# Linear attention and a rational FFN on one core: a new order table for the same instructions

## The chip, the cores and the metric

The kernel runs on one core of a Trainium2 chip. Its engines are TensorE (PE in the profile, PEld for its weight loads), VectorE (DVE), ScalarE (ACT), GpSimd (POOL) and SyncE (SP, which issues the DMAs). Each works through a queue of its own in order, and they meet at semaphores. The metric is device time in microseconds: the median of 3 runs, 544.45 us before (541.43, 544.45 and 544.65).

## The reference

```python
# attention: r, k, v (4, 8, 768, 48); w, u (8, 48)
for t in range(S):
    cur = np.einsum('bhd,bhe->bhde', u[None] * kt, vt)
    y[:, :, t] = np.einsum('bhd,bhde->bhe', rt, state + cur)
    state = w[None, :, :, None] * state + np.einsum('bhd,bhe->bhde', kt, vt)
# FFN over x = y as 3072 tokens x 384
h = x @ w_in                                   # 384 -> 2048
P = a[0] + a[1] * h + a[2] * h**2 + a[3] * h**3
Q = 1.0 + np.abs(b[0]) * np.abs(h) + np.abs(b[1]) * h**2
return (P / (Q + 1e-06)) @ w_out               # 2048 -> 384
```

The weights w_in and w_out arrive as 64-bit floats, so they are converted on the chip.

## The kernel before

**Attention.** The 3072 tokens are 24 blocks of 128; two blocks make a pair (m = 0 to 11). For a block n the kernel loads r, k and v (`rh`, `kh`, `vn`), forms the bonus term (`m`: r*k, times u, summed to `dt`, times v), scales k and r by powers of w (`wkn`, `wrn`), transposes them on PE (L513) and copies them out (`kt`, `rt`). For a pair PE forms `kv` (L562), the masked products `a` (L541, `av` after the mask of L549) and `y` in two parts (L591: with the state, then with `av` and v). DVE adds y to `m` (L607, two halves for each block); PE transposes the sum (`x`, L619), and it is kept as a high and a low half (`xth`, `xtl`).

**Weights.** They come in 28 pieces, loaded to `sti` and `sto`: in each of four groups three of w_in (512 wide, "i", 512 KB) and four of w_out (384 wide, "o", 384 KB). ACT splits a piece (L392, L380, L383), DVE joins it to a single-precision `wfi` or `wfo` (L397), ACT or DVE casts the high half (L420, `whii`, `whio`), and POOL or DVE subtracts for the low half (L417, `wloi`, `wloo`).

**FFN.** A token tile is a pair's 256 tokens. Its 2048 hidden columns are eight slices of two times 128; the first two tiles share each quarter of the weights (slices 0 and 1 of tile 0, 2 and 3 of tile 1, 4 and 5 of tile 0 again, and so on), later tiles go through in one run. Slice s: PE's product `h` (L644 in three products of halves, or L650 in full precision for tile 0), then ACT (|h| L692, `w` L698, `t` L703, ln L708, exp L712), then DVE (L716, `g` high half L722, `q` L726, the remainder d L732), then the low half of g on POOL or DVE (L736), then PE's second product into `o` (L654 to L656), which takes the low half as the third of its operands. `o` is evicted at the end of a quarter or a tile (L778, L783, L785) and stored.

**What sets the order.** The kernel is cut into 2205 tasks, each a few instructions. `ORDER` is a table of their numbers: it is the program order of all engines together, and a letter behind a number picks the engine where a task may run on two (D is DVE, A ACT, G POOL, S a DMA from SP). A token such as `w1` puts a product of ones on PE, whose result is not used. `placed` reads the table and refuses an order in which a task stands ahead of what it depends on, or a buffer runs out:

```python
for tok in ORDER.split():
    if tok[0] == "w":
        order += [("warm", "P")] * int(tok[1:])
        continue
    n = names[int(tok.rstrip(ENGINES))]
    t = tasks[n]
    e = tok[-1] if tok[-1] in ENGINES else t["eng"]
```

**The scale constants.** `pro_beta` takes the absolute values of a and b on ACT (L260, L261), clamps two of them on DVE (L264, `ctmp`), takes a root through ln and exp on ACT (L265, L266) and sets four constants on DVE (L267 to L270); `pro_squares` follows with 14 tiny DVE instructions. ACT's `t` and `w` of every slice need them.

Of the kernel before, what the change touches and what calls it, by code (L numbers as in the profile page):

```python
# [48 lines left out]
69 286D 70D 71G 789 790 791 288D 283 77D 793 93 94 792 803 804 293G 294G 291 278 304 43G 284G 95 794 796 296 96 795 97 797 798
799 800G 309D 805 128 129 130 807 131 132 806 w1 324 100 101 808 102 103 298 300 301D 310 299D 810 104 801 802 78G 323 326G 329G  # L50
297G 327G 114 107 809 115 116 117 303A 811 812 813 814G 305 307 306 308 328D 108 302A 109 110 133A 118 119A 111 312 313 319 314
815 334 318 315 332 336 325 337 339G 342G 343 121 122 123 124 335A 333A 226 227 338 316D 320 321A 317 125 126A 228 340G 345 346D
341G 347 348D 149 150 322 330 351 356 352 229 230 151 816A 152 135 136 137 57G 50G 819 820 821 112D 357 354 98D 153 91D 105D 353
355 138 139 822 154D 823 826 817 818D 824 825 827 828 829 170 350S 171 349S 833 834 837 127G 113G 331G 359 360 361 172 835 173
174 344G 849 850 836 838 365 840 140D 366 212 213 863 864 384 466 142 830G 831 839 841 842 843 99D 832 844D 845 847 851 214 852
215 216 854 865 853 856 855 857 858 848D 143 866 144 868 106G 92G 120G 162G 859 860G 145 146 846D 867 870 147D 869 871 872 385
219 220 417 177 383 879 880 881 893 861 372 371 134G 883 886 873 874G 882 221 884 222 223 885 887 888 175D 889 231D 890G 894 909
895 178 897 896 179 900 910 911 180 898 912 862 875 877 876 181 217D 182D 183G 878 923 924 141G 899 901 902 913 916 914 903 904D
163 164 191 925 165 915 166 917 192 926 193 928 194 167 168A 927 891 892 905 918 906 919 195 907 908 929 930 931 932 933 184 185
155G 148G 939 940 941 953 954 186 943 946 920G 169G 921 218G 176G 934D 922 935 187 198 199 942 200 201 188 196D 202 937 938 944  # L60
945 947 948 949 950G 957 955 956 936 958 959 960 961 962 969 970 983 971 984 197G 203A 189A 985 986 988 987 989 951 963 964D 972
974 362 363D 364 990 991 952 965 967 992 993 367 368A 369 190G 204G 1001 1002 1015 1016 1033 973 976 975 977 978 968 979 966 205
206 224A 207 208 1003 1005 386G 232G 388G 994G 387G 980G 1004 1006 1007 209 1008 210D 211D 1009 1010 1019 1034 1047 370 373G
225D 1017 1022 1018 1020 1021 394 395D 1011 1023 1048 981 1024 982 995 998 999 996 1025 397S 419 1061 1012G 389G 374D 1026G 1051
1037 1049 1035 1050 1052 1054 1053 1055 1056 1057 1058G 1062 1065 1036 1063 1038 1039 1064 392 393A 1040 1041 1042 1043 1044G
1013 1014 1027 1066 1067 1068 1069 1030 1075 1076 1079 1089 1090 1103 513 1000 1070 1031 1032 1028 1071 1072G 1077 1078 1082 379
1080 1081 1083 1084 376G 375G 358G 1104 1117 1045 1118 1046 1059 1060 1073 1093 377 1091 1092 390 1096 1085 1086D 1105 1094 1095
1097 1098 380A 391D 311G 1099 1100 1107 1119 1106 1120 1110 1108 1109 1111 1112 1121 1122 1123 1074 1087 1131 1132 1133 381 418
382A 1088 1101 1102 1113 1114 1115 1134 1136 1124 1125 1126 1127 1128 1135 1137 1138 1139 1140 398 399 403 400 1116 401 396S 431
402 406 1141 378G 407 408 1129 420G 421G 409 410A 1130 1142 412 404 413 411 414 415A 430 433G 435G 441 432 442A 426 427A 422G  # L70
428 465 464 429A 416 1149 1150 1163 1164 434G 423G 424 445 450 477 1151 1152 1153 1156 451 1167 1165 1166 1168 1170 1169 1171
1172 1173 1174 436G 1143 1144A 1154 1155 1157 1158 1159 437 439 511 560 1146 1147A 1177 1178 1179 478 1148 1181 1191 1192 1205
# [1016 lines left out]
```

## Time and profile before

| | |
|---|---|
| median of 3 runs | 544.45 us (541.43 to 544.65) |
| the profiled execution | 542.21 us, of which the span is 540.4 |
| PE, PEld busy | 510.0, 490.7 us |
| DVE, ACT, POOL busy | 427.9, 404.5, 250.0 us |
| HBM read, written | 27.73, 4.72 MB |

The span goes from the first to the last instruction of the program; the profiled execution's time is 1.8 us longer. Busy time is the union of an engine's instructions. PE's products overlap in the records, so two products that follow each other closely each show a duration longer than their distance.

### The profile page before, as it was taken

How to read it: one execution, taken by the hardware profiler on the slowest of the kernel's cores; microseconds unless marked ns; L12 is line 12 of the kernel's file. 1: busy time of each engine (PE TensorE's matmuls, PEld its weight loads, DVE VectorE, ACT ScalarE, POOL GpSimd, SP SyncE). 2: the span in 40 equal slices, each digit the busy share in tenths (PEclk: the TensorE clock that was granted, in tenths of full speed). 3: DMA queues.
4: the chain of work that ended last, by engine and by line, in shares of the span. 5: the costliest groups of instructions: out<-in, count | busy, mean ns of one | idle time of the engine just before them, and what ended most of it. 6: DMA issues, size and time to landing. Idle time of an engine off the chain costs nothing.

```text
span 540.4 us, 14734 instructions
## 1 busy us (share of the span) xinstructions
PE 510.0 (94%) x6055; PEld 490.7 (91%) x6055; DVE 427.9 (79%) x708; ACT 404.5 (75%) x666; POOL 250.0 (46%) x241
## 2 busy tenths in 40 slices
PE   4758999899999999999999999999999999999995
PEld 2647988899999999999999999999999899999995
DVE  5889999899974887887796868789867785776872
ACT  5789999998864857948963857876785785788782
POOL 3669545384444662551563654235523432222331
PEclk9899999999999999999999999999999999999999
DMA  8967642240022311104304232040031000000001
GB/s 205 267 172 202 183 112 76 79 80 16 16 52 50 79 32 45 31 4 89 81 2 91 52 76 52 2 81 2 2 82 32 1 30 2 2 30 1 29 2 35
DMA packets 88492, 33.46 MB, mean 62 GB/s; under 512 B 81761, under 2 KB 84834, under 8 KB 88418
## 3 DMA queue, kind: packets, MB, share of 16 engines
q1 hardware_dynamic: 88418, 32.46, 25.4%
q8 instruction: 49, 0.80, 0.6%
q14 instruction: 25, 0.20, 0.1%
HBM read 27.73 MB, written 4.72 MB: 60 GB/s over the span
## 4 chain that ended last, share of the span: by engine, by line
PE 76%; DVE 5%; ACT 4%; DMA 1%; issue 1%; POOL 0%; DVEq 0%; POOLq 0%; ACTq 0%; SPq 0%
PE h L644 30%; PE o L654 11%; PE o L656 11%; PE o L655 11%; PE y L591 3%; PE h L650 2%; PE kv L562 2%; PE a L541 2%; PE tr L513 2%; PE tk L513 2%; PE x L619 1%; DVE q L726 1%; DVE g L722 1%; ACT w L698 1%; DVE h L716 1%
## 5 line engine op out<-in xcount | busy, mean ns | idle before, releaser
L736 POOL TENSOR_TENSOR g<-q,z 128x512 fp32r<-128x512 f32 (+1 forms) x92 | 118.5, 1289 | 234.4 <-DVE q L732 142.9
L644 PE MATMUL h<-xth,whii 128*128 128x256 f32 x528 | 151.2, 286 | 0.1
L644 PE MATMUL h<-xtl,whii 128*128 128x256 f32 x528 | 148.0, 280 | 0.0
L644 PE MATMUL h<-xth,wloi 128*128 128x256 f32 x528 | 148.0, 280 | 0.0
L654 PE MATMUL o<-whio,g 128*128 128x384 f32 x384 | 134.5, 350 | 0.0
L656 PE MATMUL o<-whio,g 128*128 128x384 f32 x384 | 130.3, 339 | 1.9 <-DVE g L736 1.9
L655 PE MATMUL o<-wloo,g 128*128 128x384 f32 x384 | 129.9, 338 | 0.0
L698 ACT ACTIVATE w<-q,off,root 128x512 f32<-128x512 f32 (+1 forms) x97 | 75.4, 779 | 48.5 <-DVE q L726 22.5
L644 PEld LDWEIGHTS h<-xth,whii 128*128 128x128 f32 x528 | 99.4, 188 | 1.7 <-DVE q L726 0.9
L644 PEld LDWEIGHTS h<-xtl,whii 128*128 128x128 f32 x528 | 99.5, 188 | 0.0
L644 PEld LDWEIGHTS h<-xth,wloi 128*128 128x128 f32 x528 | 99.4, 188 | 0.0
L722 DVE SCALAR_TENSOR_TENSOR g<-h,sig,z 128x512 fp32r<-128x512 f32 (+1 forms) x97 | 72.1, 743 | 33.7 <-ACT z L712 29.2
L716 DVE SCALAR_TENSOR_TENSOR h<-t,sig,h 128x512 f32<-128x512 f32 (+1 forms) x97 | 71.9, 743 | 15.6 <-ACT t L703 9.7
L703 ACT ACTIVATE t<-h,off,root 128x512 f32<-128x512 f32 (+1 forms) x97 | 74.3, 767 | 6.8 <-PE h L644 6.6
L726 DVE SCALAR_TENSOR_TENSOR q<-w,sig,g 128x512 f32<-128x512 f32 (+1 forms) x97 | 72.2, 744 | 6.3
L656 PEld LDWEIGHTS o<-whio,g 128*128 128x128 f32 x384 | 72.1, 188 | 3.2 <-DVE g L736 2.9
L732 DVE SCALAR_TENSOR_TENSOR q<-h,sig,q 128x512 f32<-128x512 f32 (+1 forms) x97 | 72.0, 744 | 2.7
L654 PEld LDWEIGHTS o<-whio,g 128*128 128x128 f32 x384 | 72.1, 188 | 1.0
L655 PEld LDWEIGHTS o<-wloo,g 128*128 128x128 f32 x384 | 72.3, 188 | 0.1
L692 ACT ACTIVATE q<-h 128x512 f32<-128x512 f32 (+1 forms) x97 | 56.2, 584 | 20.7 <-PE h L644 19.7
L712 ACT ACTIVATE z<-z,lnb 128x512 f32<-128x512 f32 (+1 forms) x97 | 69.7, 719 | 2.2
L708 ACT ACTIVATE z<-w,lnb 128x512 f32<-128x512 f32 (+1 forms) x97 | 66.0, 680 | 6.9 <-POOL g L736 2.6
(141 smaller groups left out, 664.9 us busy)
## 6 DMA issues: line engine op xcount, KB each, us to landing
sti<-in_moe_w_in_dram SPq DMA_DIRECT2D x12, 512.0 KB, 5.1
sto<-in_moe_w_out_dram SPq DMA_DIRECT2D x16, 384.0 KB, 3.8
rh<-in_r_dram SPq DMA_DIRECT2D x24, 192.0 KB, 3.5
kh<-in_k_dram SPq DMA_DIRECT2D x24, 192.0 KB, 4.0
vn<-in_v_dram SPq DMA_DIRECT2D x24, 192.0 KB, 4.4
out_dram<-os SPq DMA_DIRECT2D x24, 192.0 KB, 2.1
vo<-in_v_dram SPq DMA_DIRECT2D x10, 96.0 KB, 3.9
wraw<-in_w_dram SPq DMA_DIRECT2D x1, 1.0 KB, 2.5
```

The lines of the kernel that those rows point to most:

```text
L644: nc.tensor.matmul(o, w_[nm][:, c], x_[:, cc], start=(n == 0), stop=(n == 3 * NCC - 1))
L654: nc.tensor.matmul(o, hi, w_["hi"], start=first, stop=False)
L655: nc.tensor.matmul(o, hi, w_["lo"], start=False, stop=False)
L656: nc.tensor.matmul(o, lo, w_["hi"], start=False, stop=last)
L698: nc.scalar.activation(g["w"], w_, AF.Square, scale=RB, bias=KB)
L703: nc.scalar.activation(g["t"], g["h"], AF.Square, scale=RA, bias=KA)
L712: nc.scalar.activation(g["z"], g["z"], AF.Exp, scale=-1.0, bias=lnb[:, 1:2])
L716: nc.vector.scalar_tensor_tensor(g["h"], g["t"], KAP, g["h"], op0=ALU.add, op1=ALU.mult)
L722: nc.vector.scalar_tensor_tensor(g["hi"], g["h"], c0, g["z"], op0=ALU.add, op1=ALU.mult)
L726: nc.vector.scalar_tensor_tensor(g["q"], g.get("w", g["q"]), qe, g["hi"].bitcast(F32), op0=ALU.add, op1=ALU.mult)
L732: nc.vector.scalar_tensor_tensor(g["d"], g["h"], c0, g["q"], op0=ALU.add, op1=ALU.subtract)
L736: e.tensor_mul(g["lo"], g["d"], g["z"])
```

## The change

Only the table `ORDER` is replaced. All tasks and their instructions stay, with two kinds of exception that the table itself sets: where a task may run on two engines, its letter may differ, and there are 12 tokens for a product of ones instead of 4. Of the whole program's choices, v's half copies go from 11 on ACT, 3 on DVE and 10 as a DMA to 9, 3 and 12; the casts of the high halves of weights from 10 on ACT and 18 on DVE to 6 and 22; the low halves of weights from 25 on POOL and 3 on DVE to 27 and 1; the low halves of g from 92 and 5 to 91 and 6; the scaling of k from 21 and 3 to 18 and 6. Nearly every task's place in the order is another one. The list of loads, which was r of block 0, w, two weight pieces, k of block 0, u, a weight piece, r and k of block 1, a weight piece, is now a weight piece, w, two weight pieces, k of both blocks, r of block 1, a weight piece, r of block 0, u. The new table was searched under a planner's model in which DVE and POOL are served in order of arrival at a port that they share.

```diff
 ORDER = """
-234 0 35 12 13 14 16 18 15 17 20 19 21 5 4 7 22 23 27 44 45 46 47 58 233 59 60 61 1 10 24 25 3 243 30 28 48 236G 11 238G 239 6
...
+58 59 0 35 60 7 w1 12 13 14 16 61 44 45 15 27 4 18 17 20 19 37 233 3 6 241 28 62 21 46 47 48 22 25 23 242 245 246 248G 63A 38 39
...
```

**At the scale constants, DVE.** y0 is the first pair's y, m1 the second block's sum, x0 and x1 the two transposes, wfi1_0 and wfo1 joins of weight pieces. Before:

```order
L607 TENSOR_TENSOR m1_205<-y0_1_325,m1_205 128x4x48
L607 TENSOR_TENSOR m1_205<-y0_0_324,m1_205 128x4x48
L420 COPY xth0_425<-x0_398 128x3x128
L420 COPY xth0_425<-x1_427 128x3x128
L397 SCALAR_TENSOR_TENSOR wfi1_0_439<-cp7_433,upi1_0_436 128x512
L264 TENSOR_SCALAR ctmp_96<-cabs_95 128x2
```

In the change:

```order
L607 TENSOR_TENSOR m1_185<-y0_1_325,m1_185 128x4x48
L397 SCALAR_TENSOR_TENSOR wfo1_414<-cp4_408,upo1_410 128x384
L264 TENSOR_SCALAR ctmp_96<-cabs_95 128x2
L267 MEMSET sqs_429 128x1
L268 MEMSET sqs_429 128x1
L269 MEMSET lnb_87 128x1
L270 MEMSET lnb_87 128x1
L607 TENSOR_TENSOR m1_185<-y0_0_324,m1_185 128x4x48
L420 COPY xth0_440<-x0_402 128x3x128
L420 CAST whio1_446<-wfo1_414 128x384
L420 COPY xth0_440<-x1_442 128x3x128
```

The clamp (ctmp) and the four constants now stand ahead of the last sum of m1 and of both copies of x; the 14 instructions of `pro_squares` follow the join of wfi1_0 in both.

**From d of slice 0 (q0, L732) on, DVE.** st1 is the second pair's state, vo1 its copy of v, wfo7 and wfo5 joins, kt and rt the copies of transposed k and r. Before, up to d of slice 1:

```order
L732 SCALAR_TENSOR_TENSOR q0_516<-h0_509,sig_97,q0_516 128x512
L420 COPY st1_109<-kv1_0_544 112x384
L397 SCALAR_TENSOR_TENSOR wfo7_609<-cp13_602,upo7_604 128x384
L420 COPY rt_106<-tr3_629 112x512
L573 TENSOR_TENSOR st1_109<-kv1_1_545,st1_109 112x384
L420 COPY kt_105<-tk3_624 112x512
L716 SCALAR_TENSOR_TENSOR h1_531<-t1_606,sig_97,h1_531 128x512
L397 SCALAR_TENSOR_TENSOR wfi1_2_638<-cp9_617,upi1_2_621 128x512
L722 SCALAR_TENSOR_TENSOR g1_674<-h1_531,sig_97,z1_619 128x512
L726 SCALAR_TENSOR_TENSOR q1_598<-w1_611,sig_97,g1_674 128x512
L732 SCALAR_TENSOR_TENSOR q1_598<-h1_531,sig_97,q1_598 128x512
```

In the change the first 12 rows of that stretch; eight more follow (the second half copies of vo1, a cast, r*k of block 5, and g, q and d of slice 1 among them) before d of slice 1 is done:

```order
L732 SCALAR_TENSOR_TENSOR q0_518<-h0_451,sig_97,q0_518 128x512
L736 TENSOR_TENSOR g0_563<-q0_518,z0_526 128x512
L397 SCALAR_TENSOR_TENSOR wfi1_1_587<-cp8_554,upi1_1_577 128x512
L420 COPY vo1_111<-vn2_569 64x192
L420 COPY vo1_111<-vn3_547 64x192
L716 SCALAR_TENSOR_TENSOR h1_499<-t1_633,sig_97,h1_499 128x512
L420 COPY st1_109<-kv1_0_591 112x384
L420 CAST whio8_637<-wfo8_531 128x384
L573 TENSOR_TENSOR st1_109<-kv1_1_592,st1_109 112x384
L397 SCALAR_TENSOR_TENSOR wfo5_686<-cp11_642,upo5_645 128x384
L549 TENSOR_TENSOR av_107<-a1_0_651,mask_81 128x512
L397 SCALAR_TENSOR_TENSOR wfo7_722<-cp13_649,upo7_689 128x384
```

The low half of g0, two half copies of v and a cast of a weight's high half have come in, the copies of kt and rt have gone to ACT, and the masks (L549) of the second pair now stand ahead of d of slice 1.

**Ahead of the transpose of x20, DVE.** m20 and m21 are the sums of the eleventh pair, y10 its y. Before, from the d of slice 70 on:

```order
L716 SCALAR_TENSOR_TENSOR h71_5858<-t71_6075,sig_97,h71_5858 128x512
L607 TENSOR_TENSOR m21_5325<-y10_0_5910,m21_5325 128x4x48
L490 TENSOR_TENSOR rh0_100<-rh0_100,wrn_90 128x8x48
L494 TENSOR_TENSOR m23_6117<-rh1_102,kh2_104 128x384
L607 TENSOR_TENSOR m20_5376<-y10_1_5911,m20_5376 128x4x48
L722 SCALAR_TENSOR_TENSOR g71_6125<-h71_5858,sig_97,z71_6121 128x512
L716 SCALAR_TENSOR_TENSOR h72_6002<-t72_6127,sig_97,h72_6002 128x512
L726 SCALAR_TENSOR_TENSOR q71_5886<-w71_6078,sig_97,g71_6125 128x512
L732 SCALAR_TENSOR_TENSOR q71_5886<-h71_5858,sig_97,q71_5886 128x512
L607 TENSOR_TENSOR m21_5325<-y10_1_5911,m21_5325 128x4x48
L607 TENSOR_TENSOR m20_5376<-y10_0_5910,m20_5376 128x4x48
```

In the change:

```order
L716 SCALAR_TENSOR_TENSOR h70_5855<-t70_6014,sig_97,h70_5855 128x512
L607 TENSOR_TENSOR m20_4994<-y10_1_5918,m20_4994 128x4x48
L607 TENSOR_TENSOR m21_5587<-y10_1_5918,m21_5587 128x4x48
L607 TENSOR_TENSOR m21_5587<-y10_0_5917,m21_5587 128x4x48
L607 TENSOR_TENSOR m20_4994<-y10_0_5917,m20_4994 128x4x48
L722 SCALAR_TENSOR_TENSOR g70_6102<-h70_5855,sig_97,z70_6016 128x512
```

The four sums now stand together behind one L716; before, a scaling, a product r*k and four slice steps lay between them.

## Rows read from the trace of the kernel before

**Rows 1.** The first part of the page: busy time of each engine, its share of the span and its instructions.

```profile
PE 510.0 (94%) x6055; PEld 490.7 (91%) x6055; DVE 427.9 (79%) x708; ACT 404.5 (75%) x666; POOL 250.0 (46%) x241
```

**Rows 2.** Busy time by stretch: the stretch in us, its length, then busy us (and instructions) of PE, PEld, DVE, ACT and POOL, the mean granted clock of PE, the DMA share and GB/s.

```profile
0.00:22.00 22.00, 12.00 (x220) 9.36 (x220) 14.85 (x30) 15.26 (x30) 11.49 (x27) 1.00 0.96 234
22.00:30.00 8.00, 7.05 (x55) 5.89 (x56) 5.55 (x10) 3.02 (x10) 5.77 (x7) 0.57 0.99 230
30.00:48.00 18.00, 10.78 (x198) 8.81 (x196) 16.62 (x43) 17.55 (x34) 12.57 (x13) 1.00 0.64 160
48.00:80.00 32.00, 30.77 (x480) 28.19 (x480) 31.48 (x57) 31.05 (x56) 19.31 (x18) 1.00 0.62 167
80.00:105.00 25.00, 22.36 (x128) 20.69 (x129) 22.47 (x37) 23.06 (x41) 11.53 (x10) 1.00 0.32 91
105.00:534.00 429.00, 426.40 (x4975) 417.43 (x4974) 336.89 (x533) 313.45 (x499) 189.37 (x169) 1.00 0.17 36
```

**Rows 3.** Who waited for whom, PE's own waits: the engine and line that waited, what it waited for, us in total, times, the longest.

```profile
PE h L650 <- DVE wfo L397: 3.0, 1, 3.0
PE tk L513 <- DVE q L732: 2.6, 1, 2.6
PE y L591 <- issue: 2.2, 3, 1.1
...
PE o L656 <- DVE g L736: 1.9, 2, 1.0
PE x L619 <- DVE m L607: 1.8, 2, 1.0
```

**Rows 4.** The timeline from 24 to 31 us, of DVE, of ACT and of POOL: start, duration, engine, line, operation, out<-in, shape, and in brackets the idle time before it with what ended it.

```profile
27.64 1.94 DVE L264 TENSOR_SCALAR ctmp<-cabs 128x2 f32<-128x2 f32 x1
...
30.28 0.17 DVE L277 RECIPROCAL sqs<-root 128x2 f32<-128x2 f32 x1
...
24.30 0.51 ACT L420 CAST whio<-wfo 128x384 fp32r<-128x384 f32 x1 [2.17 <-DVE wfo L397]
...
29.61 0.17 ACT L265 ACTIVATE sqs<-ctmp 128x2 f32<-128x2 f32 x1 [2.78 <-DVE ctmp L264]
...
27.60 0.99 POOL L499 TENSOR_TENSOR m<-m,ub 128x384 f32<-128x384 f32 x1
28.55 0.99 POOL L494 TENSOR_TENSOR m<-rh,kh 128x384 f32<-128x384 f32 x1
```

**Rows 5.** The timeline from 60 to 69 us: two casts of the same form on DVE, and what POOL ran beside the second.

```profile
60.98 0.41 DVE L420 CAST whii<-wfi 128x512 fp32r<-128x512 f32 x1
...
66.64 1.10 DVE L420 CAST whii<-wfi 128x512 fp32r<-128x512 f32 x1
...
66.17 2.70 POOL L417 TENSOR_TENSOR wloi<-wfi,whii 128x512 fp32r<-128x512 f32 x2
```

**Rows 6.** DVE's instructions of the first 105 us, grouped by line and form: line, operation, names, form and count, then busy us, mean ns of one, and idle time before them.

```profile
L716 DVE SCALAR_TENSOR_TENSOR h<-t,sig,h 128x512 f32<-128x512 f32 x11 | 8.2, 746 | 1.0 <-ACT t L703 1.0
...
L420 DVE CAST whii<-wfi 128x512 fp32r<-128x512 f32 x9 | 5.8, 651 | 0.0
...
L736 DVE TENSOR_TENSOR g<-q,z 128x512 fp32r<-128x512 f32 x3 | 3.1, 1032 | 0.0
...
L420 DVE CAST whio<-wfo 128x384 fp32r<-128x384 f32 x8 | 2.9, 373 | 0.0
...
L420 DVE COPY rt<-tr 112x512 f32<-112x512 f32 x3 | 2.1, 684 | 0.3 <-PE tr L513 0.3
L420 DVE COPY kt<-tk 112x512 f32<-112x512 f32 x3 | 2.0, 680 | 0.0
...
L785 DVE TENSOR_SCALAR os<-o,sig 128x384 f32<-128x384 f32 x3 | 1.8, 606 | 0.0
...
L417 DVE TENSOR_TENSOR wloi<-wfi,whii 128x512 fp32r<-128x512 f32 x1 | 1.2, 1223 | 0.0
...
L490 DVE TENSOR_TENSOR rh<-rh,wrn 128x384 f32<-128x384 f32 x1 | 0.7, 704 | 0.0
```

**Rows 7.** The same grouping over the whole run, three forms on DVE and one on ACT.

```profile
L508 DVE TENSOR_TENSOR m<-vn,dt 128x384 f32<-128x384 f32 x5 | 4.1, 817 | 0.0
...
L420 DVE COPY vo<-vn 64x192 f32<-64x192 f32 x6 | 2.8, 497 | 0.1
L494 DVE TENSOR_TENSOR m<-rh,kh 128x384 f32<-128x384 f32 x5 | 2.8, 550 | 0.0
...
L420 ACT CAST whio<-wfo 128x384 fp32r<-128x384 f32 x7 | 3.4, 506 | 2.2 <-DVE wfo L397 2.2
```

**Rows 8.** The timeline around the transpose of x20, of DVE and of PE.

```profile
423.01 0.75 DVE L732 SCALAR_TENSOR_TENSOR q<-h,sig,q 128x512 f32<-128x512 f32 x1
423.68 0.61 DVE L607 TENSOR_TENSOR m<-y,m 128x192 f32<-128x192 f32 x2
...
423.02 0.28 PE L644 MATMUL h<-xtl,whii 128*128 128x256 f32 x1
423.14 0.28 PE L644 MATMUL h<-xth,wloi 128*128 128x256 f32 x1
424.44 0.52 PE L619 MATMUL x<-ident,m 128*128 128x128 f32 x3 [1.01 <-DVE m L607]
```

**Rows 9.** The timeline of DVE at the d of slices 0 and 1.

```profile
39.79 0.75 DVE L732 SCALAR_TENSOR_TENSOR q<-h,sig,q 128x512 f32<-128x512 f32 x1
...
46.30 0.75 DVE L732 SCALAR_TENSOR_TENSOR q<-h,sig,q 128x512 f32<-128x512 f32 x1
```

More of the change, by code (lines that the diff above doesn't have):

```diff
@@ L49 @@
[L49 to L72, printed above, removed]
@@ new lines @@
+811 812 813 312 313 318 347 334 319 314 348A 340G 345 346A 315 316A 111 104 119D 814G 815 320 335D 321D 317 121 325 122 123 124
+338 351 226 227 322 134G 266G 356 357 125 105D 228 229 230 112D 149 150 151 152 817 50G 819 820 823 821 822 824 352 329G 126D
+330 331G 153 354 818D 353 355 98D 342G 343 344G 833 479 120G 113G 127G 231D 350S 135 136 137 825 826 349S 359 366 360 361 365
+138 139 827 828 829 830G 834 835 849 850 837 840 385 170 171 212 836 172 838 863 864 99G 92G 106G 173 851 839 816D 853 852 174
@@ new lines @@
+1436 1449 575G 499G 1467 1469 1472 1468 1470 1471 1473 1474 1475 585A 584S 586 591 565 576G 538S 620 547 549 554 548 592 582
+583D 563G 569 1377 606 608G 580 581A 1450 567 618 714 619 607 631S 632S 550 570A 588 568A 587 553 577D 578 551D 552 555 556A
+579D 1479 1480 1483 1481 557 589 1497 590 594 609D 614 1462 1463 566D 611D 612 596 600 595 615A 1486 601 1482 1484 1485 1487
+1488 597 598A 613G 1498 1511 1512 1464 621G 1476 1477 599 1489 622D 610G 616 617D 1499 1500 1502 1501 1504 1525 1503 1515 1505
@@ new lines @@
+1538 676 713 677D 1551 1596 1552 593G 1564 1565 657G 669G 663 1570 1587 1589 1572 1590 1591 1592 700 671G 1573 679A 1575 1576
+1577 644 645D 1599 646 1613 1614 1627 1566 1578 1597 1615 1598 1600 1617 1601 1616 1618 1619 664D 1602 1603 656D 1620 1604 1605
+1606 1621 1622 1623 699 702D 674 675A 1579 1580 1593 1628 1594 680 1607 1608D 1609 701 1629 1631 1630 685 1634 1632 1633 1635
+1636 1610 1611D 1637 686 678A 1641 1642 1655 1643 1656 1624 1638 1645 1648 1644 1659 1646 1657 1647 1658 1660 1661 1649 1662
@@ L126 @@
+2062 2079 2064 2065 2080 2082 2066 2067 2068 2069 2070 2091 2092 2093 2043 2105 2106 2107 2083 2044 2057 2058 2071 2094 2084
+2085 2086 2087 2088 2096 2109 2097 2095 2098 2099 2100 2108 2101 2102 2074 2075A 2076 2072A 2073 2119 2120 2089 2090 2110 2111
[3 rows of a table added]
+2185 2191 2194 2192 2193 2195 2196 2197 2198 2174 2186 2187 2199 2200A 2201 2202 2203A 2204
 """
```

115 lines of the change are left out of this document (62 added, 53 removed), and 6 rows, old and new, of the table ORDER.

## The prediction

> **What bounds the kernel now.** Read the busy times first [rows 1]: TensorE (PE) works for 510.0 of 540.4 us, so a change that alters no instruction can win at most the 30 us in which PE has nothing to do, some 6 of them behind its last product (what the windows below leave over), where the result is evicted and stored. Then see where that idle time lies [rows 2]: PE idles 10.0 us in the first 22, 1.0 in the next 8, 7.2 in the next 18, 1.2 and 2.6 in the two windows up to 105 us, and 2.6 in the whole remainder up to 534 us. So 22 of the 24.6 us ahead of PE's end fall into the first 105 us. There the weights are converted, the first three pairs of blocks go through the attention, and two token tiles share each quarter of the weights; VectorE (DVE) and ScalarE (ACT) are busy for 31.5 and 31.1 of the 32 us from 48 to 80. The front is bound by these two queues, and the rest by PE. Third, ask what PE waited for [rows 3]: DVE's joins of weight pieces (3.0), its elementwise steps (2.6, 1.9 and 1.8), and its own instruction supply, which the profile calls "issue" (2.2). Nothing on this list is an arithmetic limit of PE; each is a place in an order.
>
> So the new table is worth what it does at three places: the start, DVE's queue up to 105 us, and the few late waits. The sum is made against the profiled execution: 542.21 us, that is its span of 540.4 and 1.8 around it. It lies 2.2 below the median of 544.45, whose runs go from 541.43 to 544.65; I add the difference to the median. A measurement of this kernel can tell about 1% from no change, 5.4 us.
>
> **Term A, the start.** In before the scale constants are a stumbling block [rows 4]. The two-element DVE instruction of L264 took 1.94 us, where its neighbours of that size take about 0.17; its time covers two GpSimd (POOL) instructions, from 27.60 and from 28.55, and it ended as the second did. So it waited about 1.8 us for a port that both engines use, and ACT stood 2.78 us behind it. Earlier, ACT stood 2.17 us in front of a cast whose join was still queued on DVE. In the new order the L264 instruction comes earlier on DVE, ahead of the cast of whio1, and the next POOL instruction needs that cast: POOL has nothing to run, and the 1.8 us should go. The cast on which ACT stood is DVE's own now, so the 2.2 us go as well. Gain: up to 3.9. Against it stands the list of loads. Ahead of and with the last k or r block of the first pair, 2176 KB were loaded before (three weight pieces of 512, 384 and 512 KB and four blocks of 192 KB); now 2688 KB, since all four first pieces come first and r of block 0 is last. At 234 GB/s [rows 2] the extra 512 KB are 2.2 us by which the first pair's attention can start later. Either may be hidden: the first by ACT's backlog, which decided the next step anyway, the second by DVE, which had other work between. Ends: -3.9 and +2.2. I take the middle, -0.9.
>
> While the L264 instruction waits for ACT (its input is ACT's), five things queue behind it on DVE: the last sum of the first pair, both copies of x, the cast of whio1 and the next join; the first FFN product waits for the two copies. That cost is inside the +2.2: if ACT arrives 1 us late, that product is 1 us late.
>
> **Term B, DVE's queue in the first 105 us.** I list what DVE must do up to the join of the last piece that slice 12 needs (wfi3_2), the last point before 105 us at which PE waited for a join. 20 instructions stand there now that did not before: 4 half copies of v (0.50 each), 2 products r*k (0.55), 2 with u (as much), 1 with v (0.82) [rows 7], 6 casts of an output piece (0.37), 1 of an input piece (0.65), 2 low halves of g (1.03), 1 eviction (0.61) and 1 copy of rt (0.68) [rows 6]: 2.0+1.1+1.1+0.8+2.2+0.7+2.1+0.6+0.7 = 11.3. 14 are gone: 3 casts of input pieces, 1 of an output piece, 1 low half of a weight piece (1.22), 1 low half of g, one scaling each of k and r (0.70), 2 copies of kt and 3 of rt (0.68), 1 product of L716 (0.75) [rows 6]: 2.0+0.4+1.2+1.0+1.4+3.4+0.7 = 10.1. Back to back each overlaps the next by 0.08 (the step of 0.75 at 423.01 is followed at 423.68 [rows 8]), so 9.7 against 9.0: **+0.7**. These means contain the waits for the port as before had them. If DVE is late it is PE's wait for the third product of a slice (the low half) that ends last; ACT is next. ACT's queue up to its counterpart gets 9 instructions and loses 13, casts and copies of about 0.5 [rows 7], so it is 1 to 2 us shorter and I cost it at nothing.
>
> Between the ends of d of slice 0 and of slice 1, DVE's queue grows from 9 instructions in between to 18 (the order rows show the first ones). In before that stretch was 40.5 to 47.1 us [rows 9]. I expect slice 1's second half some 3 us later than now, and nothing of it at the end: the additions are the same masks, joins and copies that in before followed d of slice 1, and PE's first product of slice 2, which needs them all, is where the two orders meet again.
>
> **The port inside B.** The casts show it [rows 5]: one of a 512-wide input piece took 0.41 us, another 1.10, because a POOL instruction was running when it came; it ran as that one ended. Up to wfi3_2 DVE had 23 instructions with two SBUF operands or a copy between SBUF tiles; now it has 33. Of the 23, the 9 casts of input pieces lost 9 x (0.65-0.41) = 2.2 us to it [rows 5, 6]. The ends for the ten more are 0 each (POOL idle, as at the new L264) and one whole POOL instruction, about 1.0: 0 to +10. I take nothing beyond the means above.
>
> The Trainium skill, page "SBUF — State Buffer", section "Who interferes with whom", says that the shared pair is an exclusive lock: whoever issues first holds it for its whole instruction, and the other fully blocks. The casts agree with this; L264, which sat through two POOL instructions, waited longer than it allows. By that rule an arriving instruction waits on average half a POOL instruction when POOL is busy (19.3 of 32 us [rows 2]), an estimate of 0.3, and ten more cost +3.0: the sum would be +1.8, or 546.3 us.
>
> **Term C, eight more warm-up products.** The table holds 12 of them now instead of 4, all ahead of slice 2. A 256-column product follows the last by 0.12 us [rows 8]; eight of half the columns cost under 1.0, twice that at the lower clock level (PE had a mean granted clock of 0.57 from 22 to 30 us [rows 2]). All stand where PE waits for DVE, whose work hides them: 0, and up to +2 without that cover.
>
> **Term D, the late waits.** Of the 2.6 us after 105, one is an order's fault [rows 8]: the transpose of x20 stood 1.01 us, because DVE had the sums of the pair spread over two slices' steps (the d of slice 71 from 423.01 ran ahead of the last two sums). In the new order the four sums follow one product of L716 directly: 0.75 and twice 0.61 for two of them together [rows 8] make 2.0 us, with four half-slice products of PE, 36 x 0.12 = 4.3, to hide them. That wait goes: **-1.0**. The rest is "issue" [rows 3] and stays or moves. In the new order I found no place after slice 12 where the row durations of a slice's elementwise chain come within 1 us of the PE work that stands over it.
>
> Sum: -0.9 + 0.7 + 0 - 1.0 = **-1.2**, so 543.3 us at the median.
>
> **Rivals.** (1) Faster: the start keeps its whole gain. Then -3.9; ACT decides the front instead of DVE, with a queue about 1.1 shorter; and -1.0 for x20: -6.0, 538.4 us. For it speaks that the waits of [rows 4] are real stalls with nothing behind them; against it that DVE was busy for 98% of 48 to 80 us. (2) Slower: the port. If DVE's 33 two-operand instructions meet POOL as L264 did, each hit costs 1 us or more. Its place is the run of casts beside POOL's low halves of the weights, 50 to 105 us. About 7 hits more than the means contain lift the sum to +5.9, 550.3 us; from there on it decides. For it: 1.94 and 1.10 in before, and 33 chances against 23; against it: POOL often waits for the very cast. (3) The order is new and PE's waits only change places: that is my forecast, and its spread is some 4 us either way. (4) The clock: if PE's new pauses bring a second stretch at the half level like that of 22 to 30 us, the 7.1 us of work there would again run at about half speed: +3.5, 546.8 us, still within the 1% band.
>
> **How the numbers follow.** Forecast 0.64 with rival 4 at 0.05 beside it, rival 1 at 0.17, rival 2 at 0.14. Within 1% (539.0 to 549.9) is then 0.69, faster 0.17, slower 0.14. With the unknown ends of A (-3.0 and +3.1 from my value) and of the port, the range that leaves out no more than two in ten is 538.4 to 549.5.
>
> **What would show it.** In the profile after: L264 on DVE below 0.3 us; ACT without a 2 us wait for a join near 24 us; slice 1's d some 3 us later than 47.1; PE idle up to 105 us between 20 and 24 us; no wait of x20 for the sums; DVE casts averaging below 0.7 us for input pieces. I am wrong if PE's idle up to 105 us changes by over 4 us, if new PE waits of more than 2 us in all come up after 105, or if the casts' mean passes 0.9.

## The result and the profile after

| | before | after |
|---|---|---|
| median | 543.55 us (9 runs, 541.43 to 546.2) | 548.78 us (9 runs, 548.26 to 550.02) |
| ratio | | 1.009 (95% interval 1.0065 to 1.0114) |
| profiled execution, its span | 542.21, 540.4 | 549.2, 547.5 |

The new table is 0.9% slower, 5.2 us. The forecast was 1.2 us faster; the time lies in the stated range, the sign is wrong. The two profiled executions are 7.0 us apart, more than the medians, since that of before is one of its faster ones. A second set of runs of the same kernel (`after_again`, below) gave 1.0105 (1.0049 to 1.0161).

The busy times of the page, against [rows 1]:

```profile
PE 517.2 (94%) x6063; PEld 495.0 (90%) x6063; DVE 426.5 (78%) x715; ACT 404.6 (74%) x660; POOL 246.3 (45%) x236
```

PE is the engine that got longer, by 7.2 us, and the span grew by 7.1. Its idle time did not: its last product ends at 542.2, so 25.0 us are idle ahead of that, where it was 24.6. The products are the same but for eight small ones. They ran longer. The stretches of [rows 2], and two that single out the low clock:

```profile
0.00:22.00 22.00, 11.97 (x163) 8.75 (x165) 12.79 (x25) 13.21 (x25) 8.31 (x22) 1.00 0.98 226
22.00:30.00 8.00, 4.45 (x106) 3.37 (x101) 5.03 (x17) 5.74 (x15) 2.43 (x3) 0.66 0.85 172
30.00:48.00 18.00, 14.15 (x183) 11.54 (x182) 16.25 (x38) 15.10 (x28) 15.68 (x16) 0.87 0.64 169
48.00:80.00 32.00, 28.99 (x464) 25.78 (x464) 29.18 (x53) 26.27 (x46) 18.91 (x18) 0.89 0.48 135
80.00:105.00 25.00, 21.13 (x124) 19.66 (x125) 23.96 (x39) 22.93 (x41) 10.08 (x10) 1.00 0.33 97
105.00:541.00 436.00, 435.34 (x5028) 425.04 (x5027) 339.26 (x546) 320.23 (x507) 190.91 (x170) 1.00 0.19 39
...
24.50:34.50 10.00, 6.36 (x45) 4.74 (x37) 7.51 (x33) 6.80 (x16) 5.57 (x7) 0.50 0.83 173
48.50:55.00 6.50, 6.50 (x104) 5.95 (x102) 4.61 (x9) 4.07 (x8) 2.37 (x3) 0.50 0.23 72
```

The third number from the right is the granted clock. It is 0.50, the 1.2 GHz level, from 24.5 to 34.5 and again from 48.5 to 55. In half-microsecond windows the low level adds up to 17.1 us in the first 62 us, against 6.8 in before [rows 2]. PE was busy for 13.4 of the 17.1 us and for 6.0 of the 6.8. The 7.4 us more would take about half as long at the full level, so they are worth some 3.5 us. The column does not show all: ahead of its first change it reads 1.00, but by the durations of products PE ran at the low level's rate until about 21 us, in before until about 16 (next fences). And from 48 to 80 us DVE and ACT, which in before were busy for all but half a microsecond and one microsecond, now idle 2.8 and 5.7 us. PE's own waits, against [rows 3]:

```profile
PE o L656 <- DVE g L736: 3.8, 2, 2.1
PE x L619 <- DVE xth L420: 2.1, 1, 2.1
...
PE h L644 <- DVE q L726: 1.3, 1, 1.3
```

Where the time came in can be read from the starts of four of PE's products, which both orders have:

| profiled execution | to slice 0 | slice 0 to slice 2 | slice 2 to the second product of slice 10 | from there to the end |
|---|---|---|---|---|
| before | 27.2 | 28.8 | 53.6 | 430.8 |
| after | 30.7 | 31.0 | 57.0 | 428.8 |
| difference | +3.5 | +2.2 | +3.4 | -2.0 |

**To slice 0.** PE and DVE, against [rows 4]:

```profile
17.51 1.99 PE L541 MATMUL a<-rt,kt 48*64 48x64 f32 x64
19.27 1.90 PE L562 MATMUL kv<-vn,kh 64*64 64x48 f32 x64
...
29.12 0.90 PE L619 MATMUL x<-ident,m 128*128 128x128 f32 x3 [2.06 <-DVE xth L420]
30.67 0.80 PE L650 MATMUL h<-xth,wfi 128*128 128x256 f32 x1 [0.65 <-DVE xth L420]
```

```profile
27.46 0.17 DVE L264 TENSOR_SCALAR ctmp<-cabs 128x2 f32<-128x2 f32 x1 [0.80 <-ACT cabs L261]
28.11 0.06 DVE L267 MEMSET sqs<- 128x1 f32 x1 [0.48 <-ACT root L266]
...
28.50 0.56 DVE L420 COPY xth<-x 128x384 f32<-128x384 f32 x1
```

In before the first pair's products were:

```profile
15.22 1.44 PE L541 MATMUL a<-rt,kt 48*64 48x64 f32 x64
...
16.89 1.14 PE L562 MATMUL kv<-vn,kh 64*64 64x48 f32 x64
```

The first pair's `a` starts 2.3 us later than in before (17.51 against 15.22). L264 takes 0.17 us instead of 1.94, as forecast. But DVE stands 0.80 and 0.48 us for ACT there, with the last sum of the pair and both copies of x behind it; that sum's y was complete at 25.1, and PE stands 2.06 us at the second transpose. `a` and `kv` of the first pair take 1.99 and 1.90 us; they took 1.44 and 1.14, and the 64 products of `kv` take 1.14 wherever they run without a wait later (next view, at 58.84).

**Slice 0 to slice 2.** PE, then ACT and DVE behind it:

```profile
46.36 1.16 PE L541 MATMUL a<-rt,kt 48*64 48x64 f32 x62 [1.76 <-DVE st L420]
...
48.30 1.89 PE L591 MATMUL y<-st,rt 48*64 48x48 f32 x30 [0.43 <-DVE av L549]
...
50.61 0.52 PE L655 MATMUL o<-wloo,g 128*128 128x384 f32 x1
```

```profile
57.55 0.33 PE L655 MATMUL o<-wloo,g 128*128 128x384 f32 x1
...
58.84 1.14 PE L562 MATMUL kv<-vn,kh 64*64 64x48 f32 x64
...
61.66 0.39 PE L644 MATMUL h<-xth,whii 128*128 128x256 f32 x1 [0.43 <-DVE xtl L633]
```

```profile
53.30 0.59 ACT L420 COPY kt<-tk 112x512 f32<-112x512 f32 x1 [2.40 <-PE tk L513]
```

```profile
50.23 0.69 DVE L549 TENSOR_TENSOR av<-a,mask 128x512 f32<-128x512 f32 x1 [1.23 <-PE y L591]
...
55.29 1.15 DVE L607 TENSOR_TENSOR m<-y,m 128x192 f32<-128x192 f32 x4 [0.82 <-PE y L591]
...
57.43 2.66 DVE L420 CAST whio<-wfo 128x384 fp32r<-128x384 f32 x1
```

PE stands 1.76 us within `a`, then has small products, and its clock falls. The product of 384 columns takes 0.52 us at 50.61 and 0.33 at 57.55, and ACT and DVE now wait for PE (2.40, 1.23, 0.82). Then a cast takes 2.66 us; POOL beside it:

```profile
56.82 0.83 POOL L611 TENSOR_TENSOR st<-st,w 112x384 f32<-112x384 f32 x1
57.60 1.29 POOL L417 TENSOR_TENSOR wloi<-wfi,whii 128x512 fp32r<-128x512 f32 x1
58.85 1.01 POOL L499 TENSOR_TENSOR m<-m,ub 128x384 f32<-128x384 f32 x1
```

The cast came while the first ran, and ended 0.22 us behind the third. The low halves of x2 and x3 and PE's slice 2 follow it directly.

**Slice 2 to slice 10.** Three waits of PE: 2.10 and 1.7 for the low halves of slices 3 and 7 (L736 on DVE), 1.3 at slice 10. In DVE's queue ahead of the first of them:

```profile
75.50 1.14 DVE L420 CAST whio<-wfo 128x384 fp32r<-128x384 f32 x1
...
78.00 1.32 DVE L420 CAST whii<-wfi 128x512 fp32r<-128x512 f32 x1
...
80.03 0.72 DVE L736 TENSOR_TENSOR g<-q,z 128x512 fp32r<-128x512 f32 x1
```

**From slice 10 to the end** the new table wins 2.0: the late "issue" wait of y is gone, and x20, against [rows 8], doesn't wait:

```profile
428.01 0.49 PE L619 MATMUL x<-ident,m 128*128 128x128 f32 x3
```

### The profile page after: what moved, and what is told of

Read it like the earlier page. It is cut to its first block, busy times and chain, and to the rows that moved or that the text cites. A ratio compares the mean times of both kernels' runs of the same rounds, so it can differ in the third digit from the quotient of the medians.

```text
span 547.5 us, 14737 instructions
## 1 busy us (share of the span) xinstructions
PE 517.2 (94%) x6063; PEld 495.0 (90%) x6063; DVE 426.5 (78%) x715; ACT 404.6 (74%) x660; POOL 246.3 (45%) x236
## 4 chain that ended last, share of the span: by engine, by line
PE 78%; DVE 0%; ACT 0%; issue 0%
PE h L644 33%; PE o L654 11%; PE o L656 11%; PE o L655 11%; PE y L591 4%; PE kv L562 2%; PE a L541 2%; PE tr L513 2%; PE tk L513 1%; PE x L619 1%; PE h L650 1%; DVE q L726 0%; DVE g L722 0%; ACT q L692 0%; ACT os L783 0%; ACT kt L420 0%
## 5 line engine op out<-in xcount | busy, mean ns | idle before, releaser
L736 POOL TENSOR_TENSOR g<-q,z 128x512 fp32r<-128x512 f32 (+1 forms) x91 | 117.8, 1295 | 220.1 <-DVE q L732 144.3
L722 DVE SCALAR_TENSOR_TENSOR g<-h,sig,z 128x512 fp32r<-128x512 f32 (+1 forms) x97 | 72.1, 743 | 36.7 <-ACT z L712 32.1
L716 DVE SCALAR_TENSOR_TENSOR h<-t,sig,h 128x512 f32<-128x512 f32 (+1 forms) x97 | 71.6, 744 | 16.6 <-ACT t L703 11.8
L732 DVE SCALAR_TENSOR_TENSOR q<-h,sig,q 128x512 f32<-128x512 f32 (+1 forms) x97 | 72.0, 743 | 2.4
```

What stands on the lines that cost most here:

```text
L716: nc.vector.scalar_tensor_tensor(g["h"], g["t"], KAP, g["h"], op0=ALU.add, op1=ALU.mult)
L722: nc.vector.scalar_tensor_tensor(g["hi"], g["h"], c0, g["z"], op0=ALU.add, op1=ALU.mult)
L732: nc.vector.scalar_tensor_tensor(g["d"], g["h"], c0, g["q"], op0=ALU.add, op1=ALU.subtract)
L736: e.tensor_mul(g["lo"], g["d"], g["z"])
```

## The experiments

All times are medians; ratios are to the kernel before on the same chip. The edits are in `ORDER` alone: numbers moved, or tokens for products of ones added. Tables joined from two (`front_b`, `front_a`, `start_b`) keep no token of the second. One slip runs through the expectations: where they name slice 12 and times of 56 to 62 us, the place is the start of slice 2.

### In which part the loss arises

`front_b` and `front_a` join the tables at place 310, `start_b` at place 150.

> The changed kernel unaltered, timed on the same chip as the three kernels beside it, and a second profile of it. Expected 548.8 us, 5.2 over the kernel before. If its second stretch at half clock (48.4 to 55.3 us in the first profile) is a property of the order, it is there again at the same place; if not, it lies elsewhere or is missing, and the time tells what it is worth: in the first result executions with a mean granted clock of 0.994 took 550.0 and those with 0.98 took 548.3 to 549.4, so a theory that the half clock makes the loss expects the opposite of that.

> The first 310 places of the old table (to the start of slice 12's neighbours, about 60 us), then all other tasks in the order of the new table. If the whole loss arises in the first 62 us (slice 12 starts at 61.7 instead of 56.0): 542, a little under before because x20 no longer waits. If the stretch from 62 to 105 us loses its own 2.7 us (the new waits of PE at slices 3, 7 and 10): 545. If the new front is innocent: 548.

> The reverse: the first 310 places of the new table, then all other tasks in the order of the old one. If the whole loss arises in the first 62 us: 549. If 2.7 of it comes behind: 546.5. If the front is innocent: 543.5.

> The first 150 places of the old table (through the first product of slice 0, about 30 us), then all other tasks in the order of the new one. Slice 0 starts at 27.2 us in the profile of the old kernel and at 30.7 in that of the new one. If the loss sits in the start and is carried on: 3 us less than the new table, 545.5. If it arises between 30 and 62 us (second half clock, what stands ahead of slice 12): 548 to 549. With the whole front of the old table to slice 12 it was 543.2.

| | ratio (95%) | median | to slice 0 | 0 to 2 | 2 to 10 |
|---|---|---|---|---|---|
| `after_again` | 1.0105 (1.0049 to 1.0161) | 548.98 | 31.1 | 31.0 | 56.9 |
| `front_b` | 0.9998 (0.9967 to 1.003) | 543.22 | 26.8 | 28.8 | 55.8 |
| `front_a` | 1.0186 (1.0126 to 1.0246) | 554.0 | 31.6 | 30.9 | 60.6 |
| `start_b` | 1.003 (1.0 to 1.0061) | 546.92 | 26.7 | 32.1 | 57.7 |

The first 310 places make the loss: with the old ones the new remainder costs nothing, and the old remainder behind the new front is worse than the new one, since it adds a wait of 3.70 us at slice 3's first product. The start alone, 4 us earlier at slice 0, gives back some 3 us (ratio 1.003 for 1.009), although the granted clock is 0.50 from 37 to 50.5 us there. In `after_again` the low clock lies at the same places (25 to 35 and 48.5 to 55.5).

### The port

```diff
 ch11_late: the cast of piece 11
-104 119D 814G
+104 814G
...
-227 322
+227 322 119D
```

> The new table with one number moved: DVE's cast of the high half of piece 11 (whio, 128x384) stands behind the low halves of x2 and x3 instead of ahead of the copies of rt and x3. In the profile of the changed kernel it took 2.66 us instead of 0.35, from 57.43 to 60.08, while POOL ran three instructions back to back to 59.86; PE's first product of slice 12 started at 61.66, 0.05 after the last of the steps behind it. Theory of the port: slice 12 starts 2.3 us earlier and the end comes 2 us earlier, 546.5 to 547. Rival, that something else of the new order would hold slice 12 anyway (the states, ACT's queue) or that the gain is lost in the waits of slices 3 and 7: 548.8.

Measured: 549.63, ratio 1.0111 (1.0051 to 1.0172). The cast took 0.35 us at its new place and slice 2's first product no longer waited for DVE: it followed PE's own work, at 60.60, 30.1 behind slice 0 instead of 31.0. Then PE stood 1.32 us in the y of the next pair, and slice 2 to slice 10 took 59.0 us instead of 57.0. In this order, taking away the longest single delay by the port won nothing at the end.

### The clock

```diff
 warm_second
-300 301A
+w10 300 301A
...
-305 117
+w24 305 117
 warm_first: w10, w10, w14, w30 and w10 ahead of 261, 267, 270, 274 and 789
 warm_both: both. warm_all: both, and w50 for the first w1. warm_start: that alone
 f20_early
-305 117
+802 305 117
...
-306 802 131
+306 131
```

> The new table with 34 more products of ones: 24 between the second product of slice 0 and the a of the second pair, where PE stood 1.76 us at 46.36, and 10 ahead of tr3, where it stood 0.76 at 40.46. Nothing else moves. Theory of the clock: the second stretch at half clock (48.4 to 55.3) does not come, since PE is no longer idle just before it; the y of the second pair, its two products and tk4, which took 8.0 us there, take 4.7, and ACT, which stood 2.4 us for tk4, goes on earlier: the time falls by 2 to 3.3, to 545.5 to 547. Rival, that DVE and the port set slice 12's start whatever PE's clock is: 548.9 even without the stretch. If the stretch stays, this run tells nothing on the price.

> The new table with 74 more products of ones, in the waits of PE ahead of ys0, y0, x0, x1 and slice 0 (21 to 31 us), some 4 us of work at full clock. Theory: the first stretch at half clock (24.5 to 34.7, 10 us, against 22.4 to 29.2 before) shortens or goes; the two products of slice 0 take 2.9 instead of 5.1 us, and the chain to slice 12 that runs over them and PE's products behind them gets about 2 us shorter: 547. Rival, that the constants' wait on DVE and ACT (x1 stood 2.06 us) or DVE's later queue decides: no change, 548.9, or up to 1 us slower where the added products stand in the way.

> Both sets of added products. If the half clock explains most of the 5.2 us and both stretches go: 543.5 to 545. If the two gains aren't additive, since DVE's queue holds behind the first: 546 to 547. If the clock isn't on the path: 548.9.

> The new table with one number moved: the second half of slice 0's second product stands ahead of the a of the second pair instead of behind its ys. It ran at half clock from 50.13 to 52.41; its operands were there at 42.8, and PE stood idle for 1.76 us at 46.36. By the order alone PE is 1.3 us earlier at tk4 and y1 (a row of the same products at full clock took 1.3), so 548.9 - 1.3 = 547.6; if besides the second stretch at half clock goes, as the theory of the clock has it, another 2: 545.6. Rival, that DVE's queue (d of slice 1 at 54.5) or the port holds the next step: 548.9.

> The new table with 50 products of ones instead of 1 at the start (2 to 8 us, where PE waits for its first tables). In the profile of the changed kernel PE's products run at half their later rate until 21.2 us (64 products of kv0 took 1.90, of kv1 without a wait 1.14; the granted clock is shown as 1.00 there), in that of the old one until 15.6. Theory: PE comes to full rate before tk0, a0 and kv0 take 2.2 instead of 3.9 us together, and the first pair is 1.5 to 2.5 us earlier; the end follows by up to that, 546.5 to 548. Rival: ACT's and DVE's work ahead of the constants decides the first FFN product, 548.9.

> The new table with all three sets of added products (start, first waits, ahead of tr3 and a1). By the theory of the clock the gain of the two later sets together (3.6 us, 545.3 against 548.9) is kept and that of the start is added: 543 to 544.5. Rival, that the front is then bound by DVE and ACT: 545.3.

| | ratio (95%) | median | clock column low, 22 to 62 us | cast of piece 11 | 0 to 2 |
|---|---|---|---|---|---|
| after | 1.009 (1.0065 to 1.0114) | 548.78 | 17.1 | 2.66 | 31.0 |
| `warm_second` | 1.0056 (1.0028 to 1.0085) | 548.44 | 0 (some 14 by durations) | 0.56 | 28.4 |
| `warm_first` | 1.0082 (1.0053 to 1.0112) | 550.14 | 6.8 | 2.93 | 30.2 |
| `warm_both` | 1.0004 (0.9976 to 1.0033) | 545.28 | 0 | 0.57 | 27.1 |
| `f20_early` | 1.0068 (1.0046 to 1.0089) | 548.23 | 17.1 | 0.59 | 29.6 |
| `warm_start` | 1.009 (1.0059 to 1.0121) | 550.15 | 20.8 | 2.65 | 31.0 |
| `warm_all` | 1.0076 (1.0046 to 1.0105) | 549.0 | 3.4 | 3.10 | 29.1 |

The last three columns are from one profiled execution each. With both sets of added products, which do no work that is used, the new table takes the old one's time. In its profile, of an execution that took 547.4 us, the clock is at the full level where it had fallen:

```profile
22.00:30.00 8.00, 7.25 (x169) 6.45 (x168) 5.14 (x18) 6.51 (x16) 1.83 (x2) 1.00 0.85 180
30.00:48.00 18.00, 15.65 (x243) 13.20 (x244) 16.69 (x40) 15.78 (x29) 16.36 (x16) 1.00 0.69 182
```

and ACT, which stood 2.40 us for `tk`, stands 0.23:

```profile
50.45 0.58 ACT L420 COPY kt<-tk 112x512 f32<-112x512 f32 x1 [0.23 <-PE tk L513]
```

From slice 0 to slice 2 it needs 27.1 us, 3.9 less than the changed kernel and 1.7 less than before.

But the clock is not all that differs. The cast of 2.66 us, that of piece 11, is short in `warm_both` (first fence) and long in `warm_all` (second), which has the same two sets and 49 products more at the start:

```profile
54.44 0.68 DVE L397 SCALAR_TENSOR_TENSOR wfi<-cp,upi 128x512 int32<-128x512 int32 x1
55.03 0.57 DVE L420 CAST whio<-wfo 128x384 fp32r<-128x384 f32 x1
55.52 0.68 DVE L420 COPY rt<-tr 112x512 f32<-112x512 f32 x1
```

```profile
54.62 0.68 DVE L397 SCALAR_TENSOR_TENSOR wfi<-cp,upi 128x512 int32<-128x512 int32 x1
55.22 3.10 DVE L420 CAST whio<-wfo 128x384 fp32r<-128x384 f32 x1
58.25 0.68 DVE L420 COPY rt<-tr 112x512 f32<-112x512 f32 x1
```

`warm_all` was to gain more, and its gain is gone. Its clock is low from 48.5 to 52, yet at the join ahead of the cast it is only 0.2 us behind `warm_both`; behind the cast it is 2.7 us behind. So some 2 of the 3.9 us that `warm_both` wins up to slice 2 go with the cast, which the added products moved against POOL's work; that was not intended. `f20_early`, with a short cast and the low clock as before, won 1.4 there. No run parts the two at the end of the kernel.

One set alone isn't told from the changed kernel. In `warm_second` the column shows no low clock up to 62 us, but the first stretch was there. The twelve products of slice 0 took as long as at the low level, where those of `warm_both` (second row) did not, and only the second stretch is gone:

```profile
31.56 4.96 PE L650 MATMUL h<-xth,wfi 128*128 128x256 f32 x12 [0.65 <-DVE xth L420]
```

```profile
31.09 2.86 PE L650 MATMUL h<-xth,wfi 128*128 128x256 f32 x12
```

PE then stands as long as ever at slice 3, its clock falls there, from 80 to 84, and most of what was won is spent by the end (span 547.3 against 547.5). `warm_start` has the 49 products at the start alone:

```profile
0.00:22.00 22.00, 15.65 (x204) 12.68 (x204) 12.78 (x25) 12.79 (x24) 8.27 (x22) 0.70 0.95 220
22.00:30.00 8.00, 5.43 (x104) 4.59 (x104) 4.70 (x16) 6.34 (x16) 1.83 (x2) 0.50 0.87 190
```

The low level is shown from 8.5 us on, right behind the added products, where PE waits for tables and loads, and holds to 36. Up to 21 us that is what the changed kernel had too, unshown: its first `tk`, its `a` and its `kv` took 1.07, 1.99 and 1.90 us in both. So nothing was won for the first pair. `f20_early` fills the wait within `a` with real work, but another wait of 0.88 comes at `tk`, the low clock stays, and y of the next pair stands 2.16 us.

The reverse, in the old table, and the added products there:

```diff
 before_f20_late
-801 802 78G
+801 78G
...
-307 306 308
+307 306 802 308
 before_warm: w30, w8, w10, w12, w44 and w40 ahead of 22, 261, 267, 270, 803 and 298
```

> The old table with one number moved, to the place that it has in the new one: the second half of slice 0's second product stands behind the ys of the second pair instead of ahead of its a. Theory of the clock: PE's full-width work ahead of the small products of a and ys is gone, the clock falls to half for a stretch at about 45 to 52 us as with the new table, and the end comes 1.5 to 3 us later, 546 to 547. Rival, that only the waits count: PE waited 1.10 and 0.94 us at ys1 and y1, and the moved product fills the second: no change, 544.5 to 545.

> The old table with 144 more products of ones where PE stands idle: 30 ahead of its first transposes, 8 to 12 each ahead of ys0, y0 and x0, 44 ahead of the first product of slice 1 (a wait of 2.95 us) and 40 ahead of tk3 (2.61). Theory of the clock: the stretch at half clock at 22 to 29 us, and the further ones that the slower executions of the old kernel must have by their mean clock (0.979 to 0.987 in those of 544 to 547 us, 0.991 to 0.993 in those of 540 to 543), go; the median falls by 2 to 4 us, to 541, and the spread narrows. Rival, that the mean clock and the time go together for another reason, or that DVE and ACT bound the front whatever PE's clock: no change, 544 to 545.

`before_f20_late`: 545.71, ratio 1.0004 (0.997 to 1.0038). In the profile the low clock did come, behind a wait of 2.19 us at ys, and five of the six products of the moved half took 0.52 each:

```profile
47.00:51.00 4.00, 4.00 (x80) 3.47 (x80) 2.90 (x6) 3.91 (x11) 3.74 (x4) 0.57 0.38 113
```

Slice 2 started 30.8 us behind slice 0 instead of 28.8, yet the times are not told apart. The fall was about half as long as that of the changed kernel. `before_warm`: 543.25, ratio 0.9987 (0.9953 to 1.0021), also not told apart; slice 2 starts at 55.9 as before, though slice 0 comes 1.4 us earlier. The first low stretch is gone there, but the clock column reads 0.57 from 47.5 to 51.5, so the run does not show what holds slice 2. That it is DVE and ACT is argued from [rows 2].

### The casts ahead of slice 3, and the start

```diff
 warm_ports: warm_both, and the casts of pieces 19 and 14, one with its low half on POOL (176)
-174 175D 176G 142
+174 142
...
-140D 843 844D
+843 844D 175D 176G 140D
 warm_ports_loads: warm_ports, and r of block 0 (234) first, u (1), k and r of block 1 behind k of block 0
 beta_late: the scale constants
-2 8 276
+2 276
...
-275D 789
+275D 8 789
 warm_ports_beta: warm_ports and beta_late
```

> The table with the two later sets of added products (545.3 us), and besides DVE's casts of pieces 19 and 14 moved from ahead of d of slice 3 to behind its low half. In the profiles of all kernels with the new table so far they took 1.0 to 1.1 and 1.3 us instead of 0.35 and 0.42, beside POOL, and PE's second product of slice 3 waited 2.08 us for that low half. Theory of the port: that wait falls by the two casts and what they lost, 2.1 to 2.4 us, to nearly nothing, and the end comes 1.5 to 2 us earlier, 543.5. Rival: the casts meet POOL again where they stand now, or the waits at slices 7 and 10 grow by as much: 545.3.

> The new table with the two later sets of added products and the two casts moved (544.3 us), and the list of loads with r of block 0 first and u behind k of block 0, so that 2176 KB instead of 2688 stand ahead of and with the last k or r block of the first pair. By Term A of the prediction 2.2 us of the later start are the loads: 542 to 543, and slice 0 starts about 2 us earlier. Rival: ACT's and DVE's queues ahead of the constants hold slice 0: 544.3.

> The new table with one number moved: the scale constants' start (L260 to L270, on ACT and DVE) stands behind both copies of x instead of ahead of the last sum of the first pair. In the profile of the changed kernel DVE stood 0.80 us at L264 and 0.48 at L267 for ACT, with that sum, both copies and a cast queued behind it; y was there at 25.1, slice 0 started at 30.67. By the step of the prediction that put this cost inside the loads': slice 0 starts 1.5 to 2.4 us earlier, and since an earlier slice 0 was worth 2 us of 4 (start_b), the end comes 1 us earlier, 547.5 to 548. Rival: the constants then hold slice 0's t and w by as much, 548.9.

> The same move on top of the table with the added products and the two casts moved (544.3 us): 542.5 to 543.5 if it counts there, and then the new table's three repairs have taken back more than its loss; 544.3 if DVE's queue behind it holds.

| | ratio (95%) | median | to slice 0 | 0 to 2 | 2 to 10 |
|---|---|---|---|---|---|
| `warm_ports` | 0.9994 (0.9971 to 1.0017) | 544.27 | 29.3 | 27.1 | 56.1 |
| `warm_ports_loads` | 1.0 (0.9967 to 1.0033) | 544.84 | 28.7 | 27.1 | 55.7 |
| `beta_late` | 1.0074 (1.0049 to 1.0099) | 549.3 | 28.3 | 32.0 | 57.1 |
| `warm_ports_beta` | 1.0027 (1.0 to 1.0053) | 546.91 | 30.1 | 28.3 | 56.1 |

In `warm_ports` PE waits 0.83 us at slice 3 instead of 2.1, and 1.7 at slice 7 as ever; the median is 1 us below `warm_both`'s, which the intervals don't tell apart. `warm_ports_loads` did not bring the first pair forward: its `a` started at 17.25, where the kernels with the changed list of loads have 16.55 (`warm_ports`) to 18.27. But it is no clean test of the bytes. PE's wait for r, 0.82 us in `warm_ports`, is gone, while w, now third in the list, came later: DVE's first step on it stands at 6.99 instead of 5.70, and the tables that the first pair needs follow from it. `beta_late` started slice 0 2.3 us earlier, as expected, and lost it again by slice 2: the constants come later, and PE's wait within `a` grew from 1.76 to 2.38.

### A version that beats both

```diff
 before_best: before_warm, and
-735 1833
+735 740 734 1833
...
-903 904D
+903 155G 904G
...
-943 946
+943 934D 946
```

> The old table with 144 more products of ones in PE's waits of the first 41 us (which alone gave 543.25 us against 544.73, not told apart), and four of its places mended: the sums of x20 together (its wait of 1.01 us), the low half of slice 7 on POOL ahead of that of piece 15 instead of on DVE beside it (1.73 instead of 0.68 us, PE waited 0.96), the low half of slice 9 ahead of the L716 of slice 10 (PE waited 0.92). If these waits go and nothing takes their place: 2 to 3 us less than the old kernel, 541.5 to 542.5. Rival: the wait at slice 12 for its last join (0.56 us) grows by what slices 7 and 9 give, and only x20's is won: 543.5.

541.32 us, ratio 0.9932 (0.9899 to 0.9966): 0.7% faster than before, though not told apart from `before_warm`. The waits at x20 and slice 9 are gone; slice 7's stayed, and slice 12's grew, as the rival had it:

```profile
PE h L650 <- DVE wfi L397: 1.9, 1, 1.9
...
PE o L656 <- POOL g L736: 0.9, 1, 0.9
```

These waits account for some 0.6 us net; the rest of the 3.2 us is not explained by them.

## Why the prediction was wrong, point by point

**What bounds the kernel.** The reading of [rows 1 to 3] holds: what is won or lost lies in the front, and `front_b` shows it. The step that failed is the one taken from it, that PE's busy time is fixed because no instruction is altered, so that only idle time can change. The idle time stayed (24.6 and 25.0) while the busy time grew by 7.2. By rows, some 3.5 of these are work done at the low clock, 1.3 the first pair's `a` and `kv` (1.99 and 1.90 for 1.44 and 1.14), and some 0.5 eight added products; the remaining 2 are spread over the run and not accounted for. Most signs named to watch were blind to it: L264 at 0.17, no 2 us wait of ACT near 24 us, PE idle 24.3 up to 105 us, no wait of x20, all about as foretold. Two did show it: d of slice 1 ended 7.4 us later than in before instead of 3, and the casts of input pieces averaged 0.80 us, not below 0.7.

**Term A.** -0.9 was forecast, with +2.2 as the worst; slice 0 came 3.5 later and d of slice 0 1.3 (41.87 at its end, against 40.54). Both gains were there. The failed step is the sentence that put the queue behind L264 inside the loads' 2.2. It came on top: `beta_late` gives 2.3 at slice 0 by moving that one task. Its gain did not reach the end. The first pair's `a` is 2.3 us later as well, in `beta_late` still 1.5; the two overlap, since they make more than 3.5. That the loads' bytes make `a` late was argued and stays open, since `warm_ports_loads` made w later as it made r earlier.

**Term B.** +0.7 for DVE's count of instructions was beside the point, since DVE was not the bound: up to 105 us it was busy for 87.2 us, where the rows of before add up to 91.0. The failed step is "nothing of it at the end": d of slice 1 ended at 54.5 instead of the 50 expected, and slice 2, where the two orders should have met again, started 5.7 us later. The two d, against [rows 9]:

```profile
41.12 0.75 DVE L732 SCALAR_TENSOR_TENSOR q<-h,sig,q 128x512 f32<-128x512 f32 x1
...
53.72 0.75 DVE L732 SCALAR_TENSOR_TENSOR q<-h,sig,q 128x512 f32<-128x512 f32 x1
```

**The port.** I took no more than the old means. DVE's casts up to 105 us, against [rows 6]:

```profile
L420 DVE CAST whio<-wfo 128x384 fp32r<-128x384 f32 x12 | 7.2, 611 | 0.1
...
L420 DVE CAST whii<-wfi 128x512 fp32r<-128x512 f32 x6 | 4.8, 802 | 0.0
```

0.611 and 0.802 instead of 0.373 and 0.651: 12 x 0.24 + 6 x 0.15 = 3.8 us more on the casts alone, of which 2.3 lie in the one of 2.66 us and 0.8 in that of 1.14. The sentence by the Trainium skill, page "SBUF — State Buffer", section "Who interferes with whom", had put +3.0 for it as an estimate. That is near by luck, since it was meant for ten more instructions at 0.3 each. The section's rule, that whoever issues first has the shared pair for that instruction, doesn't cover the cast of 2.66 us, which sat through the rest of one POOL instruction and two whole ones. What these delays cost the end is unresolved: `ch11_late` won nothing and `warm_ports` 1 us at most, but `warm_all` and `warm_both`, 1.0076 and 1.0004, part at this cast.

**Term C.** Eight more products took some 0.5 us of PE; what they cost the end was not measured. That such products can change PE's clock, and when DVE meets POOL, was the missing half.

**Term D.** Right: x20 no longer waits, and the stretch behind slice 10 is 2.0 shorter.

**Rivals.** The fourth, a second stretch at the low clock, given 0.05 and +3.5, is what the profile shows, and `warm_both`, which fills the waits ahead of it, takes the loss back, though with the long cast gone as well. The second, the port from 50 to 105 us, is there as well.

**What stays open.** How the 5.2 us divide among the clock, the start and the port: the old start won some 3, every other repair alone 2 or less, not told apart, and only the two sets of products together brought the old time, by the clock and the cast at once. The mean clock of whole executions goes with the time for the old table (113 executions beside the experiments: medians 546.2 at 0.983 and below, 544.4 at 0.984 to 0.987, 542.0 above), but not for the new one: three of 13 had 0.993 to 0.995 and took 549.7 to 550.0, the other ten 0.979 to 0.984 and 548.3 to 549.4. `warm_second`'s profile is such an execution, with 0.994, and shows one way to it: the slow start up to 36 us is not in that mean, since the column reads 1.00 there.

## What to carry to other kernels

When only an order changes, PE's busy time is no constant: before and after, read the granted clock by stretch, with the durations of like products beside it, and ask of each pause of PE whether small products or idle time around it let the clock fall. What a low clock costs is read where other engines then wait for PE: ACT stood 2.40 us for it here, while in the old order a fall half as long cost nothing that could be told apart. Before a gain is put down to an edit, compare the long instructions of the other engines in both profiles: here one cast of DVE came and went with the edits to PE. And an instruction that waits for another engine must be priced with everything queued behind it, as a term of its own.
